# Single PSUM banks, pipelined rounding, two interleaved FFN units and decay within a chunk, in a retention block followed by a SwiGLU FFN

## The chip, the cores and the metric

One core of a Trainium2 chip. The metric is the time of one execution on the device in microseconds; a figure is the median of the runs named with it. Engines are named as in the profile: PE is TensorE (PEld its weight loads), DVE VectorE, ACT ScalarE, POOL GpSimd; SPq and ACTq are queues from which transfers are issued. A profile line gives start, duration, engine, line of the kernel, operation and tiles; in brackets stands how long the engine was idle before and what released it.

## The reference

Retention over 8 batches and 8 heads (576 positions, 64 per head), then an FFN over the 4608 tokens of 512 features. All products are fp32; the weights arrive as fp64.

```python
scores = scale * np.matmul(q, k.transpose(0, 1, 3, 2))
gamma = 1.0 - 2.0 ** (-5.0 - np.arange(H))
Dmat = np.where(rel >= 0, gamma[:, None, None] ** rel[None], 0.0)   # rel = pos_q - pos_k
x = np.matmul(scores * Dmat[None], v)            # then (B,H,S,D) -> (B*S, H*D)
xn = x / np.sqrt(np.mean(x * x, axis=-1, keepdims=True) + 1e-06) * rms_g
g = xn @ w_gate
out = (g / (1.0 + np.exp(-g)) * (xn @ w_val)) @ w_out
```

## The kernel before

A job is a batch and a pair of heads (32 jobs); a unit is 384 tokens of the FFN (12 units). An f is one of the 12 blocks of 128 of the 1536 hidden features: for each f a unit makes a gate product and a value product, and `h` is SiLU(gate) times value. `ret` holds a job's scores after the mask, `av` its values, `sd` the copies of its states (sums of k times v). An `attention_step(j)` computes scores of job j within chunks of 128 positions and per-chunk states, then the values of job j-1. FFN steps are issued between attention steps as soon as their tokens are there; a batch yields one or two units, so that attention steps come in runs where FFN work has run out. The weights (36 chunks) are rounded from fp64 words on VectorE with one step on ScalarE.

```python
psum = ctx.enter_context(tc.tile_pool(name="psum", bufs=4, space=PS))
def banks(name):                                   # two banks, one tile
    return psum.tile([P, 2, 512], F32, tag="ps", name=name)
...
def gate(u, f, hs):
    weights_to(2 * f + 4)                          # rounds chunks ahead of use
    ps = banks(f"gv_{u}_{f}")
    project(u, f, w_gate, ps[:, 0])
    t = ffn.tile([P, U], F32, tag="silu", name=f"silu_{u}_{f}", bufs=2)
    nc.scalar.activation(out=t, in_=ps[:, 0, :U], func=AF.Silu)
    hs[f] = t, ps[:, 1]                            # the value product goes to the second half
...
def attention_step(j):
    scores(j); states(j)          # PE
    values(j - 1)                 # PE, reads ret(j - 1)
    weigh(j)                      # DVE: ret = s * causal (2 buffers), sums; POOL: copies the states
    carried(j - 1)                # PE, reads the states and qT(j - 1)
    prepare(j + 2)                # DVE transposes q, k; POOL scales q and v
    load(j + 3)
...
def round_chunk(i):
    # DVE: e = exponent of hi ; ACT: e = Relu(e - 896)
    # DVE: e = min(e, 255) * 2**23 ; e = sign(hi) | e          <- need ACT's result
    # DVE: dst = mantissa of hi ; dst += lo * 2**-32           <- need nothing from ACT
    # DVE: dst = dst * 2**-20 * e
```

(Conditions on j, transfers and operands are cut.)

## Time and profile before

| | before |
|---|---|
| time, 3 runs | 1637.59 us (1637.22 to 1637.93) |
| PE / DVE / POOL busy | 84% / 23% / 8% |
| first gate product starts | 108.8 us |
| unit 0's output ends | 320.5 us |
| the value product's waits for the SiLU | 134.5 us, 139 times |

The page's lines for the busy shares and the wait stand in the prediction; the two times are read from TensorE's timeline.

```profile
L205 POOL COPY sd<-sum 64x256 f32<-64x256 f32 x64 | 26.3, 410 | 1063.2 <-DVE sum L202 1061.0
```

Read the two times as borders: up to 108.8 us TensorE has attention alone, to 320.5 us TensorE follows VectorE's rounding of weights, and after that TensorE is nearly full.

### The profile page before, as it was taken

How to read it: one execution, taken by the hardware profiler on the slowest of the kernel's cores; microseconds unless marked ns; L12 is line 12 of the kernel's file. 1: busy time of each engine (PE TensorE's matmuls, PEld its weight loads, DVE VectorE, ACT ScalarE, POOL GpSimd, SP SyncE). 2: the span in 40 equal slices, each digit the busy share in tenths (PEclk: the TensorE clock that was granted, in tenths of full speed). 3: DMA queues.
4: the chain of work that ended last, by engine and by line, in shares of the span. 5: the costliest groups of instructions: out<-in, count | busy, mean ns of one | idle time of the engine just before them, and what ended most of it. 6: DMA issues, size and time to landing. Idle time of an engine off the chain costs nothing.

```text
span 1638.6 us, 13258 instructions
## 1 busy us (share of the span) xinstructions
PE 1374.8 (84%) x5312; PEld 758.2 (46%) x5312; DVE 373.8 (23%) x772; ACT 160.4 (10%) x310; POOL 131.2 (8%) x180
## 2 busy tenths in 40 slices
PE   4555554879999999889999899889999999799998
PEld 3433221454444455555444544554444644354444
DVE  3754456241000211330000410230000300110000
ACT  0111111110000100100000100100000100100000
POOL 3320000030000100220000300120000200000000
PEclk9777775889999999999999999999999999799999
DMA  9761223150000210430000410230000100000000
GB/s 181 154 133 52 77 77 115 50 96 0 13 7 0 62 28 14 89 72 0 20 1 7 95 31 0 62 71 0 19 0 7 42 1 7 13 0 7 13 0 20
DMA packets 244349, 67.15 MB, mean 41 GB/s; under 512 B 225600, under 2 KB 238016, under 8 KB 244160
## 3 DMA queue, kind: packets, MB, share of 16 engines
q1 hardware_dynamic: 228928, 46.17, 14.0%
q10 hardware_dynamic: 15360, 20.14, 4.0%
q8 instruction: 42, 0.69, 0.2%
q14 instruction: 19, 0.16, 0.0%
HBM read 56.84 MB, written 9.44 MB: 40 GB/s over the span
## 4 chain that ended last, share of the span: by engine, by line
PE 74%; DVE 11%; ACT 6%; DMA 3%; SPq 3%; issue 2%; POOL 2%; ACTq 0%; DVEq 0%; POOLq 0%
PE gv L297 48%; PE out L322 22%; ACT silu L307 4%; SPq L116 2%; DMA kraw<-in_k_dram 2%; ACT exp L428 2%; DVE exp L432 1%; DVE ret L192 1%; DVE exp L429 1%; DVE exp L424 1%; PE s L171 1%; DVE kT L143 1%; PE av L215 1%; PE av L228 1%; ACT sq L255 1%
## 5 line engine op out<-in xcount | busy, mean ns | idle before, releaser
L297 PE MATMUL gv<-x,w_val 128*128 128x384 f32 x1152 | 427.3, 516 | 134.6 <-ACT silu L307 134.5
L297 PE MATMUL gv<-x,w_gate 128*128 128x384 f32 x1152 | 407.4, 498 | 26.8 <-DVE x L290 26.8
L322 PE MATMUL out<-w_out,h 128*128 128x512 f32 x864 | 386.5, 606 | 21.9 <-DVE w_out L442 21.9
L297 PEld LDWEIGHTS gv<-x,w_val 128*128 128x128 f32 x1152 | 215.4, 197 | 344.5 <-ACT silu L307 221.4
L297 PEld LDWEIGHTS gv<-x,w_gate 128*128 128x128 f32 x1152 | 223.6, 195 | 188.9 <-issue 25.2
L314 DVE TENSOR_TENSOR h<-silu,gv 128x384 f32<-128x384 f32 x144 | 79.8, 554 | 888.6 <-PE gv L297 888.6
L322 PEld LDWEIGHTS out<-w_out,h 128*128 128x128 f32 x864 | 165.7, 193 | 235.5 <-issue 195.9
L307 ACT ACTIVATE silu<-gv 128x384 f32<-128x384 f32 x144 | 70.7, 491 | 764.5 <-PE gv L297 739.4
L171 PE MATMUL s<-qT,kT 64*128 64x128 f32 (+1 forms) x640 | 57.4, 320 | 66.2 <-DVE ret L192 22.9
L205 POOL COPY sd<-sum 64x256 f32<-64x256 f32 x64 | 26.3, 410 | 1063.2 <-DVE sum L202 1061.0
L192 DVE TENSOR_TENSOR ret<-s,causal 128x768 f32<-128x768 f32 (+2 forms) x96 | 47.5, 542 | 167.4 <-PE s L171 166.3
L171 PEld LDWEIGHTS s<-qT,kT 64*128 64x128 f32 (+1 forms) x640 | 46.7, 212 | 80.0 <-issue 30.6
L328 ACT COPY o<-out 128x512 f32<-128x512 f32 x36 | 21.1, 586 | 376.0 <-PE out L322 376.0
L148 POOL TENSOR_TENSOR v<-v,gv 128x512 f32<-128x512 f32 x64 | 49.3, 790 | 29.2 <-DMA v<-in_v_dram 29.2
L215 PE MATMUL av<-ret,v 128*64 128x128 f32 (+1 forms) x640 | 51.1, 305 | 0.0
L145 POOL TENSOR_TENSOR qT<-qT,gq 128x576 f32<-128x576 f32 x32 | 45.0, 1405 | 56.4 <-DVE qT L143 49.9
L215 PEld LDWEIGHTS av<-ret,v 128*64 128x64 f32 (+1 forms) x640 | 42.2, 163 | 7.2 <-issue 5.9
L428 ACT ACTIVATE exp<-exp,least 128x512 f32<-128x512 uint32 x36 | 26.0, 721 | 176.1 <-DVE exp L424 176.1
L228 PE MATMUL av<-qT,sd 128*128 128x128 f32 (+1 forms) x256 | 37.1, 289 | 0.7 <-POOL sd L205 0.7
L239 ACT COPY x<-av 128x192 f32<-128x192 f32 (+1 forms) x80 | 23.4, 356 | 136.6 <-PE av L228 112.8
L228 PEld LDWEIGHTS av<-qT,sd 128*128 128x128 f32 x256 | 32.7, 200 | 3.4 <-POOL sd L205 1.1
L259 DVE TENSOR_TENSOR sq<-sq 128x768 f32<-128x768 f32 (+1 forms) x24 | 18.3, 761 | 62.6 <-ACT sq L255 62.2
(40 smaller groups left out, 359.4 us busy)
## 6 DMA issues: line engine op xcount, KB each, us to landing
qraw<-in_q_dram SPq DMA_DIRECT2D x128, 72.0 KB, 2.5
kraw<-in_k_dram SPq DMA_DIRECT2D x128, 72.0 KB, 2.7
out_dram<-o SPq DMA_DIRECT2D x36, 256.0 KB, 2.0
kn<-in_k_dram SPq DMA_DIRECT2D x64, 128.0 KB, 2.9
v<-in_v_dram SPq DMA_DIRECT2D x64, 128.0 KB, 2.8
w<-in_moe_w_gate_dram ACTq DMA_DIRECT2D x12, 512.0 KB, 3.8
w<-in_moe_w_val_dram ACTq DMA_DIRECT2D x12, 512.0 KB, 3.6
w<-in_moe_w_out_dram ACTq DMA_DIRECT2D x12, 512.0 KB, 3.5
```

The lines of the kernel that those rows point to most:

```text
L116: nc.sync.dma_start(out=t[r : r + SQ], in_=rows[i])
L145: nc.gpsimd.tensor_tensor(out=d["qT"], in0=d["qT"], in1=gq[:, hp], op=ALU.mult)
L148: nc.gpsimd.tensor_tensor(out=t, in0=t, in1=gv[:n, hp, cs].unsqueeze(3).to_broadcast([n, cs.stop - cs.start, 2, D]), op=ALU.mult,)
L171: nc.tensor.matmul(d["s"][blk][:n, e, o : o + n], lhsT=d["kT"][r, ck], rhs=d["qT"][r, ck], start=True, stop=True,)
L192: nc.vector.tensor_tensor(out=ret[:n, :, c0 * P : c0 * P + m * n].rearrange("p e (c k) -> p e c k", c=m), in0=s[blk][:n, :, o : o + m * n] ...
L215: nc.tensor.matmul(av[e * D : e * D + D, blk, o : o + n], lhsT=d["v"][:n, c, e], rhs=d["ret"][:n, e, c * P : c * P + n], start=(c in (0, A ...
L228: nc.tensor.matmul(av[:, blk, o : o + n], lhsT=sd[j % 2][:, c - 1], rhs=d["qT"][:, c * P : c * P + n], start=False, stop=(c in (AC - 1, NC ...
L297: nc.tensor.matmul(ps[:, :U], lhsT=w[:, c, f * P : f * P + P], rhs=x_of[u][:, c], start=(c == 0), stop=(c == NHP - 1),)
L307: nc.scalar.activation(out=t, in_=ps[:, 0, :U], func=AF.Silu)
L314: nc.vector.tensor_tensor(out=h, in0=t, in1=ps[:, :U], op=ALU.mult)
L322: nc.tensor.matmul(ps[s][:, :DM], lhsT=hs[f][:, s * P : s * P + P], rhs=w_out[:, f], start=(f == 0), stop=(f == NF - 1),)
L428: nc.scalar.activation(out=e.bitcast(F32), in_=e, func=AF.Relu, bias=least)
```

## The change

Its intent: gate, value, out and av each take one bank from a ring of four (scores keep two pairs), so that nothing waits for a neighbour in the same tile; the exponent of the next chunk is taken ahead, so that VectorE needn't wait for ScalarE; units 0 and 1 are interleaved from f = 6, so that TensorE has work while weights are rounded; the decay is counted from the start of each chunk, which shrinks the tables from 1152 + 20 to about 256 KB on the device side and frees SBUF for more buffers of `h` (14 to 20). To make room, `ret` goes from two buffers to one and q, k, v are prepared one step ahead, not two. Besides, the norm of a unit is issued a little later, the query scaling becomes two operations and the SiLU gets a third buffer. `LEAD` is the number of f that unit 0 is ahead, `WAHEAD` that of weight chunks loaded ahead. The core of the diff (its cuts are marked by `...`):

```diff
-    psum = ctx.enter_context(tc.tile_pool(name="psum", bufs=4, space=PS))
+    pairs = ctx.enter_context(tc.tile_pool(name="pairs", bufs=2, space=PS))
+    banks = ctx.enter_context(tc.tile_pool(name="banks", bufs=4, space=PS))
...
-        s, ret = d.pop("s"), att.tile([P, 2, S], F32, tag="ret", name=f"ret_{j}")
+        s, ret = d.pop("s"), att.tile([P, 2, S], F32, tag="ret", name=f"ret_{j}", bufs=1)
...
-            nc.vector.tensor_tensor(out=t[:, c], in0=part[:, c], in1=t[:, c - 1], op=ALU.add)
+            nc.vector.scalar_tensor_tensor(
+                out=t[:, c], in0=t[:, c - 1], scalar=gc[:, hp : hp + 1], in1=part[:, c],
+                op0=ALU.mult, op1=ALU.add,
+            )
...
-            nc.gpsimd.tensor_copy(out=sd[j % 2][r, :, r], in_=t[r])
+            nc.gpsimd.tensor_scalar(
+                out=sd[j % 2][r, :, r], in0=t[r], scalar1=gc[r, hp : hp + 1], scalar2=None,
+                op0=ALU.mult,
+            )
...
+        ps = bank(f"val_{u}_{f}")
         project(u, f, w_val, ps)
...
+        for f in range(NF):
+            yield from up(0, f)
+            if f >= LEAD:                       # LEAD = 6
+                yield from up(1, f - LEAD)
+        yield from down(0)
...
+        if j + 1 < len(jobs):
+            prepare(j + 1)
         if j + 2 < len(jobs):
-            prepare(j + 2)
+            load_kv(j + 2)
         if j + 3 < len(jobs):
-            load(j + 3)
+            load_qk(j + 3)
...
     def weights_to(n):
+            exponent(n_chunks + 1)
             round_chunk(n_chunks)               # inside: mantissa steps first, then ACT's result
-            if n_chunks + 2 < len(chunks):
-                load_chunk(n_chunks + 2)
+            if n_chunks + WAHEAD < len(chunks): # WAHEAD = 3
+                load_chunk(n_chunks + WAHEAD)
```

## The prediction

> **What bounds the kernel now.** I read the page's busy shares and 40 slices first, then the groups by line, then the timeline in four places: a steady stretch, the stretch in which the first unit's weights are rounded, a run of attention steps, and the end.
>
> ```profile
> PE 1374.8 (84%) x5312; PEld 758.2 (46%) x5312; DVE 373.8 (23%) x772; ACT 160.4 (10%) x310; POOL 131.2 (8%) x180
> PE   4555554879999999889999899889999999799998
> DVE  3754456241000211330000410230000300110000
> PEclk9777775889999999999999999999999999799999
> ...
> L297 PE MATMUL gv<-x,w_val 128*128 128x384 f32 x1152 | 427.3, 516 | 134.6 <-ACT silu L307 134.5
> L322 PE MATMUL out<-w_out,h 128*128 128x512 f32 x864 | 386.5, 606 | 21.9 <-DVE w_out L442 21.9
> ```
>
> TensorE sets the end, but not as one regime. In the first seven slices (to about 287 us) it is half busy at a clock of 0.6 to 0.8, because VectorE rounds weights; from there on it is 90% busy at a clock near 1.0. The groups name the largest wait: the value product waits 134.5 us for the SiLU. The steady timeline shows what that is:
>
> ```profile
> 458.17 2.85 PE L297 MATMUL gv<-x,w_val 128*128 128x384 f32 x8 [0.58 <-ACT silu L307]
> 460.85 2.74 PE L297 MATMUL gv<-x,w_gate 128*128 128x384 f32 x8
> 463.63 0.49 ACT L307 ACTIVATE silu<-gv 128x384 f32<-128x384 f32 x1 [5.52 <-PE gv L297]
> 464.18 2.85 PE L297 MATMUL gv<-x,w_val 128*128 128x384 f32 x8 [0.58 <-ACT silu L307]
> ```
>
> Each fp32 matmul is two records, so one product is x8. Gate and value together recur every 6.01 us. The value product needs nothing of the SiLU; it waits because both halves are one two-bank PSUM tile. The wait lists give 127 such waits of 0.58 us after 345 us, and 12 before it that sum to 60.8 us. The second kind is here:
>
> ```profile
> 159.26 0.42 DVE L424 TENSOR_SCALAR exp<-w 128x512 uint32<-128x512 uint32 x1
> 160.47 0.43 DVE L429 TENSOR_SCALAR exp<-exp 128x512 uint32<-128x512 f32 x1 [0.79 <-ACT exp L428]
> 163.33 0.42 DVE L424 TENSOR_SCALAR exp<-w 128x512 uint32<-128x512 uint32 x1
> ...
> 167.27 0.49 ACT L307 ACTIVATE silu<-gv 128x384 f32<-128x384 f32 x1 [2.76 <-DVE w_val L439]
> 167.81 4.81 PE L297 MATMUL gv<-x,w_val 128*128 128x384 f32 x8 [6.54 <-ACT silu L307]
> 172.46 2.74 PE L297 MATMUL gv<-x,w_gate 128*128 128x384 f32 x8
> ```
>
> A chunk of weights takes VectorE 4.07 us, 0.75 of it waiting for ScalarE. Two chunks, then a SiLU held behind ScalarE's weight load, then the value product, then its multiplication, run one after another: some 13.9 us for each f of unit 0. Last, attention steps in a run, warm:
>
> ```profile
> 678.72 1.42 PE L171 MATMUL s<-qT,kT 64*128 64x128 f32 x20
> 680.07 0.69 PE L181 MATMUL s<-v,kn 128*64 128x64 f32 x16
> 680.59 1.31 PE L215 MATMUL av<-ret,v 128*64 128x128 f32 x20
> 681.82 1.10 PE L228 MATMUL av<-qT,sd 128*128 128x128 f32 x8
> 682.86 1.42 PE L171 MATMUL s<-qT,kT 64*128 64x128 f32 x20
> ```
>
> A step is 4.14 us of TensorE and the next follows without a gap.
>
> **What the Trainium skill says.** "PSUM — Partial Sum Buffer", section "PSUM bank collisions raise a hardware error": two engines must not touch one bank in one quadrant together, while different banks run clean. So single-bank tiles lose this wait legally; the trace agrees that the wait (0.58) is just the SiLU (0.49) plus hand-over. "Perfetto Trace Analysis", section "Optimization Strategy": a repeated equal bubble on the engine that should be full can mean too few buffers; the 0.58 that recurs fits. "TensorE: Matmul & The Clock Gate", section "HAM oscillation": idle gaps over about 3.4 us bring the half clock back. The trace agrees: the value product takes 4.5 to 5.5 us after 6.5 us of idling, 2.85 otherwise. "SBUF — State Buffer", section "Who interferes with whom": VectorE and GpSimd share a port pair. The trace agrees in the attention start, where the same rounding operation takes 1.42 instead of 0.69 us while GpSimd runs.
>
> **The change part by part.**
>
> *Single banks.* Without the wait, eight matmuls follow at the 0.322 us seen inside a product: 2.58 us each, 5.16 for an f. The out product confirms the continuous rate (24 records in 10.3 us at 512 columns). Saving 6.01 - 5.16 = 0.85 us for each f in the steady part. ScalarE (0.49) and VectorE (0.55) per 5.16 us keep up, and a ring of four gives a bank back one whole f before it is needed. After the first stage there are 126 f left (12 x 12, less 12 of unit 0, less 6 moved forward), and some five have a norm or attention between gate and value and never waited: 121 x 0.85 = 103 us.
>
> *Rounding pipelined.* The 0.75 us wait goes: 3.32 us a chunk. The separate value bank takes the product out of the loop too. An f with two chunks then costs VectorE 6.64 + 0.3 (SiLU behind the weight load) + 0.55 = 7.5 us instead of 13.9.
>
> *Units 0 and 1 interleaved.* From f = 6 a slot holds an f of each unit, 10.3 us of TensorE against 8.1 of VectorE, so TensorE bounds it. The instruction order of the built kernel confirms this, and that one more attention step (nine, not eight) comes before the first gate.
>
> *The start, step by step.* The first gate started at 108.8 us. The tables shrink (1152 KB to 256 KB), the transposes are held to one step ahead, and one more step goes in; I set 110. f = 0 to 2, with a cold first product: 19 us, 129. f = 3 with one chunk: 6, 135. f = 4 and 5: 15, and 2 for the next unit's norm: 152. Six doubled slots: 12 x 5.16 + 1 = 63, 215. Ten chunks of w_out, in VectorE's order after the last multiplication: 33, 248, with TensorE mostly idle. Its last matmul and the two other row blocks: 22, **270**. In the kernel before, unit 0 ended at 320.5. Moreover 6 f of unit 1 (36 us at the old rate) and one attention step (4.1) are already done.
>
> *What attention pays.* `ret` goes from two buffers to one and q/k are prepared one step ahead instead of two. The built kernel shows the first multiplication of a step waiting for the value products of the step before. In a run of steps without FFN between, the loop is then: scores, states and values of the step on TensorE 3.2 us, weighing on VectorE 1.5, sums 0.95, one transpose 0.75, GpSimd's query scaling about 1.3 (1.405 for 576 columns, now 512 first), hand-overs 0.3: 8.0 us instead of 4.14. Cold, as in the first 100 us (scores 2.4, values 2.3), about 10.4. At the start VectorE and loading already held a step to about 10.5 us, so nothing is lost there. In the late part the order shows three runs, with 5 + 6 + 2 such waits: 13 x 4.6 (between warm 3.9 and cold) = 60 us. Against it stand the old kernel's own waits there (query scaling 13.4, and norm waits of about 12, as the squares leave the path of the next transpose): -25. Net **+35**.
>
> *GpSimd and VectorE details.* Two query scalings instead of one, and a scalar operand in sums and states: under 1 us a step, beside other work except in that loop.
>
> Sum: 270 + (1638.6 - 320.5) - 36 - 4 - 103 + 35 = 1480 us, 158 less.
>
> **Rivals.**
> (A) *The attention runs cost nothing.* For: they cost little now, and a loop may be broken if TensorE gets ahead by a step. Against: the wait is in the built order. Time: about 1445.
> (B) *The start stays bound by VectorE and loading.* Interleaving moves TensorE's work into the stage but takes nothing from VectorE, which has to round 36 chunks whatever the order (120 us at 3.32); if GpSimd's port or weight loading stretches a chunk back to 4, and SiLUs behind loads on ScalarE's queue stop the ring of banks, the stage ends near 305. For: ScalarE did wait 2.7 us behind loads each time. Against: with three staging buffers a load has two chunks of time, 6.6 us, against 3.6 to land. Time: about 1515.
> (C) *The bubble is replaced.* If four banks shared among gate, value, out and av bring a new wait on the multiplication, the 103 us halve: about 1530. Against: a bank has a whole f of slack.
>
> **Range and chances.** The 103 us are nearly arithmetic. The start (50 + 40 us) and the attention runs (+35) are each uncertain by some 30. Together: 1480, range 1440 to 1520. Even with half of all gains lost it is 1560, well below the 2% line at 1605. Faster 0.97, same 0.02, slower 0.01.
>
> **What would show it right or wrong.** Right: value products without any wait for the SiLU and 5.16 us per f; rounding at 3.3 us a chunk with no idle before its third step; first gate near 110, unit 0's last out near 270; TensorE's clock at 1.0 from about 155 us; a wait for query scaling or `ret` of about 4 us at each step of an attention run. Wrong: value or gate products that wait for a multiplication or copy (C), VectorE's chunks above 4 us or TensorE idle in the doubled slots (B), or attention runs at 4.1 us a step (A).

## The result, and the profile after

1505.24 us (1503.73 to 1509.79, 4 runs) against 1637.76 us before in the same rounds. The ratio is 0.9192 (95% interval 0.9169 to 0.9215). Ratios here are the mean time of one kernel's fast runs over that of the other's fast runs of the same rounds, so not quite the ratio of the medians quoted. All runs that are compared were fast (none lies over 0.6% above the fastest of its kernel).

The page of the changed kernel, in the same order as in the prediction: busy shares, slices, groups.

```profile
PE 1335.9 (89%) x5312; PEld 777.0 (52%) x5312; DVE 390.4 (26%) x772; ACT 160.8 (11%) x310; POOL 175.9 (12%) x212
PE   2557896999999995699999996599999999699999
PEclk9668995999999997899999998789999999699999
...
L307 PE MATMUL val<-x,w_val 128*128 128x384 f32 x1152 | 397.8, 489 | 3.5 <-ACT silu L317 3.0
L212 POOL TENSOR_SCALAR sd<-sum,gc 64x256 f32<-64x256 f32 x64 | 59.9, 937 | 1007.1 <-DVE sum L206 1004.2
L174 PE MATMUL s<-qT,kT 64*128 64x128 f32 (+1 forms) x640 | 68.9, 373 | 120.5 <-POOL qT L144 104.5
```

The value product's wait is gone: 134.5 us became 3.0. In its place stands a new largest wait of TensorE: the scores wait 104.5 us for GpSimd's scaled queries (18.9 before). And the copies of the states now take 937 ns each, against 410 before. The slices show where: late in the kernel the 16th, 17th, 25th, 26th and 35th have PE at only 0.5 to 0.7; these are the runs of attention steps.

The timeline of one steady stretch (start, duration, engine, line, what):

```profile
186.17 2.74 PE L307 MATMUL gate<-x,w_gate 128*128 128x384 f32 x8
188.75 2.74 PE L307 MATMUL val<-x,w_val 128*128 128x384 f32 x8
191.33 2.74 PE L307 MATMUL gate<-x,w_gate 128*128 128x384 f32 x8
193.91 2.74 PE L307 MATMUL val<-x,w_val 128*128 128x384 f32 x8
```

Starts are 2.58 us apart: 5.16 us an f where it was 6.01. The timeline of two steps in a run of attention steps is the counterpart:

```profile
594.88 2.49 PE L174 MATMUL s<-qT,kT 64*128 64x128 f32 x20 [5.01 <-POOL qT L144]
598.21 1.32 PE L225 MATMUL av<-ret,v 128*64 128x128 f32 x20
599.57 1.48 DVE L196 TENSOR_TENSOR ret<-s,causal 128x768 f32<-128x768 f32 x3 [6.69 <-PE av L225]
601.22 0.91 DVE L206 SCALAR_TENSOR_TENSOR sum<-sum,gc,s 128x64 f32<-128x64 f32 x3
602.12 0.78 DVE L139 STREAM_TRANSPOSE qT<-qraw 128x576 f32<-128x576 f32 x1
602.23 1.93 POOL L212 TENSOR_SCALAR sd<-sum,gc 64x256 f32<-64x256 f32 x2 [5.78 <-DVE sum L206]
604.25 1.54 POOL L144 TENSOR_TENSOR qT<-qT,gq 128x512 f32<-128x512 f32 x2
605.56 2.49 PE L174 MATMUL s<-qT,kT 64*128 64x128 f32 x20 [4.38 <-POOL qT L144]
```

Read it downwards: each line starts when the one above lets it. Scores and values on TensorE, then weighing (which waited for the values, `PE av L225`: the single buffer of `ret`), sums, transpose, then GpSimd's states *before* the query, then the query, then the next scores. This turn takes 10.7 us, the shortest after the first of a run; the others take up to 11.8 (first turns 9.2). In the run that the prediction shows it took 4.14 us without any wait.

Where the time went, by the borders of the stages:

| stage | before | after |
|---|---|---|
| to the first gate product | 108.8 us | 121.5 us (one more attention step in it) |
| from there to the end of unit 0 | 211.7 us | 162.3 us (six f of unit 1 in it) |
| from there to the end | 1318.1 us | 1220.1 us |

### The profile page after: what moved, and what is told of

Read it like the earlier page. It is cut to its first block, busy times and chain, and to the rows that moved or that the text cites. A ratio compares the mean times of both kernels' runs of the same rounds, so it can differ in the third digit from the quotient of the medians.

```text
span 1503.9 us, 13309 instructions
## 1 busy us (share of the span) xinstructions
PE 1335.9 (89%) x5312; PEld 777.0 (52%) x5312; DVE 390.4 (26%) x772; ACT 160.8 (11%) x310; POOL 175.9 (12%) x212
## 4 chain that ended last, share of the span: by engine, by line
PE 83%; DVE 9%; POOL 4%; DMA 2%; issue 1%; ACT 0%; ACTq 0%; SPq 0%; DVEq 0%; POOLq 0%
PE gate L307 24%; PE val L307 24%; PE out L331 24%; PE s L174 4%; PE av L225 3%; POOL sd L212 2%; DVE ret L196 2%; PE s L184 2%; POOL qT L144 2%; DVE sum L206 1%; DVE exp L475 1%; DMA v<-in_v_dram 1%; DVE exp L472 1%; DVE exp L449 1%; DVE w_out L478 0%
## 5 line engine op out<-in xcount | busy, mean ns | idle before, releaser
L307 PE MATMUL gate<-x,w_gate 128*128 128x384 f32 x1152 | 403.7, 494 | 18.4 <-DVE x L300 17.2
L307 PE MATMUL val<-x,w_val 128*128 128x384 f32 x1152 | 397.8, 489 | 3.5 <-ACT silu L317 3.0
L307 PEld LDWEIGHTS gate<-x,w_gate 128*128 128x128 f32 x1152 | 221.2, 193 | 177.0 <-issue 27.6
L307 PEld LDWEIGHTS val<-x,w_val 128*128 128x128 f32 x1152 | 219.9, 191 | 157.9 <-ACT silu L317 3.7
L323 DVE TENSOR_TENSOR h<-silu,val 128x384 f32<-128x384 f32 x144 | 79.8, 554 | 738.7 <-PE val L307 736.7
L212 POOL TENSOR_SCALAR sd<-sum,gc 64x256 f32<-64x256 f32 x64 | 59.9, 937 | 1007.1 <-DVE sum L206 1004.2
L174 PE MATMUL s<-qT,kT 64*128 64x128 f32 (+1 forms) x640 | 68.9, 373 | 120.5 <-POOL qT L144 104.5
L317 ACT ACTIVATE silu<-gate 128x384 f32<-128x384 f32 x144 | 70.7, 492 | 611.8 <-PE gate L307 598.7
L196 DVE TENSOR_TENSOR ret<-s,causal 128x768 f32<-128x768 f32 (+2 forms) x96 | 47.4, 549 | 251.8 <-PE av L225 249.3
L144 POOL TENSOR_TENSOR qT<-qT,gq 128x512 f32<-128x512 f32 x64 | 54.9, 877 | 13.3 <-DVE qT L139 10.8
L225 PE MATMUL av<-ret,v 128*64 128x128 f32 (+1 forms) x640 | 54.0, 318 | 0.1
L225 PEld LDWEIGHTS av<-ret,v 128*64 128x64 f32 (+1 forms) x640 | 45.3, 172 | 6.9 <-issue 6.9
L184 PE MATMUL s<-v,k 128*64 128x64 f32 x512 | 31.4, 291 | 0.1
```

The lines of the kernel that those rows point to most:

```text
L144: nc.gpsimd.tensor_tensor(out=t, in0=t, in1=gq[:, hp, :n].unsqueeze(1).to_broadcast([P, m, n]), op=ALU.mult)
L174: nc.tensor.matmul(d["s"][blk][:n, e, o : o + n], lhsT=d["kT"][r, ck], rhs=d["qT"][r, ck], start=True, stop=True,)
L184: nc.tensor.matmul(d["s"][1][e * D : e * D + D, 0, SC + c * D : SC + c * D + D], lhsT=d["k"][:, c, e], rhs=d["v"][:, c, e], start=True, st ...
L196: nc.vector.tensor_tensor(out=ret[:n, :, c0 * P : c0 * P + m * n].rearrange("p e (c k) -> p e c k", c=m), in0=s[blk][:n, :, o : o + m * n] ...
L212: nc.gpsimd.tensor_scalar(out=sd[j % 2][r, :, r], in0=t[r], scalar1=gc[r, hp : hp + 1], scalar2=None, op0=ALU.mult,)
L225: nc.tensor.matmul(av[blk][e * D : e * D + D, o : o + n], lhsT=d["v"][:n, c, e], rhs=d["ret"][:n, e, c * P : c * P + n], start=(c in (0, A ...
```

## The experiments

Twelve kernels ran, in three groups of four; each group shares its runs of the kernel before (medians 1640.44, 1640.81, 1639.99 us; the third reuses those of the first). The second group (e5 to e8) ran on another chip, so it is best compared by ratio. All gave the correct result; each time is the median of 4 runs.

| run | time | ratio to before (95%) |
|---|---|---|
| e1 before + single banks only | 1482.49 | 0.9044 (0.9017 to 0.9071) |
| e2 changed, units not interleaved | 1520.90 | 0.9273 (0.9250 to 0.9297) |
| e3 changed, two buffers of ret | 1455.62 | 0.8871 (0.8849 to 0.8893) |
| e4 changed, plain states | 1489.02 | 0.9074 (0.9054 to 0.9095) |
| e5 changed, no pipelining over chunks | 1502.49 | 0.9157 (0.9137 to 0.9177) |
| e6 changed, attention buffers of before | 1440.27 | 0.8779 (0.8764 to 0.8794) |
| e7 two ret, out by weight | 1436.28 | 0.8754 (0.8738 to 0.8770) |
| e8 all | 1424.07 | 0.8686 (0.8663 to 0.8709) |
| e9 changed, rounding wholly as before | 1519.32 | 0.9259 (0.9236 to 0.9283) |
| e10 best | 1414.64 | 0.8631 (0.8606 to 0.8656) |
| e11 before + three small edits | 1434.90 | 0.8753 (0.8732 to 0.8775) |
| e12 changed again | 1505.40 | 0.9178 (0.9152 to 0.9203) |

**e1: one part alone.** The ring of four single banks put into the kernel before, nothing else.

```diff
-    psum = ctx.enter_context(tc.tile_pool(name="psum", bufs=4, space=PS))
+    pairs = ctx.enter_context(tc.tile_pool(name="pairs", bufs=2, space=PS))     # scores
+    single = ctx.enter_context(tc.tile_pool(name="banks", bufs=4, space=PS))    # all else
-        ps = banks(f"gv_{u}_{f}")
-        hs[f] = t, ps[:, 1]
+        ps = bank(f"gate_{u}_{f}")          # and bank(f"val_{u}_{f}") in value()
```

> The kernel before with one part of the change alone: scores keep two pairs of banks, everything else (gate, value, out, av, norm) goes to a ring of four single banks; attention, rounding and order of units as before. Theory (the single banks pay through the value product's wait): 127 waits late x 0.85 = 108 us, and in unit 0 nine slow f go from 13.8 to about 9.0 us (two chunks of 4.07, 0.3, 0.55): 43 us more. About 1487 us, so FASTER than the whole change (1505), because the change pays for its gains in the attention steps. Rival (the banks' wait was only part, and interleaving and pipelined rounding carry the gain): about 1530, the 108 us alone or less.

Measured 1482.49 us. This part alone takes 158 us off, and is 23 us faster than the whole change. So the banks carry the gain, and the rest of the change taken together costs more than it brings. In e1's page the value product no longer waits for the SiLU at all:

```profile
L298 PE MATMUL val<-x,w_val 128*128 128x384 f32 x1152 | 397.1, 488 | 5.8 <-DVE w_val L443 5.8
```

Unit 0's slow f recur every 9.0 us, as expected, and unit 0 ends at 276.6 us instead of 320.5. The edit has a price too: scores have two pairs to themselves, where four were shared, and their waits for the weighing before (`<-DVE ret`) rise from 22.9 to 39.2 us.

**e2: interleaving undone.**

```diff
-    LEAD = 6
+    LEAD = 12
```

> The changed kernel with units 0 and 1 one after the other (the lead set to 12, which also gives the ring of h 14 buffers). Theory: in the doubled slots TensorE set the time (10.3 us each, 62), without them VectorE does (7.5 us an f, 45), and the six f of unit 1 (31 us) come later: plus 14 us, and a colder clock in the stage adds some: 1515 to 1525. Rival (interleaving is worth the whole six f, since the stage is bound by VectorE whatever is done): plus 31, 1536.

Measured 1520.90 us, 16 us more than the changed kernel (1505). The theory's 14 holds, the rival's 31 does not: of the six f moved forward only about half is gain, since the doubled slots lengthen the stage (unit 0's output starts at 227.4 us with them, at 207.1 without).

**e3: two buffers of ret.**

```diff
-att.tile([P, 2, S], F32, tag="ret", name=f"ret_{j}", bufs=1)
+att.tile([P, 2, S], F32, tag="ret", name=f"ret_{j}", bufs=2)
```

> The changed kernel with two buffers of ret again, nothing else. Theory (the loop of a lone attention step runs through ret): weighing no longer waits for the value products; the next transpose is then held by its own buffer (released by the last product of the step), so 1.5 us of the loop's 11.4 go, over 8 early and 13 late steps: minus 25 to 30, about 1478. Rival (the loop is held by preparing one step ahead and GpSimd, ret does not matter): within 5 us of the changed kernel.

Measured 1455.62 us: 50 us less, the sign and mechanism of the theory with nearly twice its size. From the timeline of TensorE in e3's counterpart run of steps, three lines that don't follow one another directly:

```profile
567.50 2.49 PE L174 MATMUL s<-qT,kT 64*128 64x128 f32 x20 [2.34 <-POOL qT L144]
576.20 1.42 PE L174 MATMUL s<-qT,kT 64*128 64x128 f32 x20 [2.98 <-POOL qT L144]
584.30 2.25 PE L174 MATMUL s<-qT,kT 64*128 64x128 f32 x20 [1.72 <-POOL qT L144]
```

In the late runs a step now recurs every 8.0 to 9.5 us instead of 10.7 to 11.8 (the first of a run every 7.2 instead of 9.2). Two things account for more than the estimate: of the 13 scores that wait, five ran in 1.42 us, where in the changed kernel all took 2.48 or 2.49; and the start gained 9 us (first gate at 112.5 instead of 121.5 us). That the shorter idling brought the clock back is a reading of these traces, not a test. In the lists of waits after 300 us the 13 waits for queries fall from 63.4 to 34.2 us.

**e4: states copied plainly.** The factor of a whole chunk is moved into the tables: values carry gamma to (128 - position), the mask gamma to -128 for each head. The result is the same.

```diff
-    t = ..., pairs.T[None] ** -pos[:, None, None], rows**P
+    t = ..., pairs.T[None] ** (P - pos)[:, None, None], rows**P
-                in1=causal[:n, :n].unsqueeze(1).unsqueeze(1).to_broadcast([n, 2, m, n]),
+                in1=causal[:n, hp, :, :n].unsqueeze(2).to_broadcast([n, 2, m, n]),
-            nc.gpsimd.tensor_scalar(out=sd[j % 2][r, :, r], in0=t[r], scalar1=gc[r, hp : hp + 1], ...)
+            nc.gpsimd.tensor_copy(out=sd[j % 2][r, :, r], in_=t[r])
```

> The changed kernel with the factor of a whole chunk moved out of GpSimd's copy of the states: the value table carries gamma to (128 - position) and the causal mask gamma to -128, so that the states are copied plainly as in the kernel before; same result. Theory (the multiplication with a scalar operand, 0.94 us against 0.41 for the copy, delays the query scaling that each attention step waits for): 1.1 us x 21 steps = 23 us, about 1482. Rival (GpSimd's time lies beside other work): no change. The loop without it should be near 10.3 us.

Measured 1489.02 us, 16 us less. The copies take 394 ns, and the late steps recur every 10.1 to 10.6 us (10.3 expected); the scores' waits fall from 104.5 to 79.2 us. The total falls less than 23 us; part of it was probably lost at the start, where new waits for loading (4.6 us) appear and the first gate comes 5 us earlier, not 9.

**e5: no pipelining over chunks**, and **e9: the old order inside a chunk as well.**

```diff
 e5:
-            exponent(n_chunks + 1)
+            exponent(n_chunks)
             round_chunk(n_chunks)
-    WAHEAD = 3
+    WAHEAD = 2
 e9, besides: the two steps on e (min/mult, sign) ahead of the two steps on dst again
```

> The changed kernel with a chunk's exponent taken just before its rounding again, and two chunks loaded ahead instead of three. Theory (each chunk then costs VectorE 0.75 us of waiting for ScalarE, which counts only where VectorE sets the time: the five chunks of f 3 to 5 and the ten of w_out; the attention start and the doubled slots have room): plus 11 us, about 1516. Rival (all chunks lie on the path): 0.75 x 36 = 27 us, about 1532.

> The run without pipelining again, and now the order of the steps inside a chunk as in the kernel before too (the step that needs ScalarE's result comes second, not fourth). In the run without pipelining the chunk stayed at 3.19 us, since two steps that need nothing from ScalarE already covered its 0.72 us. Theory (the gain of rounding is all in the order inside a chunk): a chunk goes to 4.05 us, and over five chunks of f 3 to 5 and ten of w_out that is 15 x 0.8 = 12 us: about 1515. Rival (the attention start pays as well): up to 12 + 9 x 0.8 = 20 us, 1523; or nothing, 1503, if the stage's slack takes it.

e5 missed: 1502.49 us, no slower than the changed kernel (the intervals overlap). Lines of one chunk in e5, then in e9, up to the first step of the next, say why; the page calls the steps by the tile that they write.

```profile
237.69 0.42 DVE L449 TENSOR_SCALAR exp<-w 128x512 uint32<-128x512 uint32 x1
238.02 0.42 DVE L465 TENSOR_SCALAR w_out<-w 128x512 uint32<-128x512 uint32 x1
238.14 0.72 ACT L453 ACTIVATE exp<-exp,least 128x512 f32<-128x512 uint32 x1 [2.47 <-DVE exp L449]
238.47 0.69 DVE L469 SCALAR_TENSOR_TENSOR w_out<-w,w_out 128x512 f32<-128x512 uint32 x1
239.08 0.42 DVE L472 TENSOR_SCALAR exp<-exp 128x512 uint32<-128x512 f32 x1
240.87 0.42 DVE L449 TENSOR_SCALAR exp<-w 128x512 uint32<-128x512 uint32 x1
```

```profile
237.10 0.42 DVE L449 TENSOR_SCALAR exp<-w 128x512 uint32<-128x512 uint32 x1
237.56 0.72 ACT L453 ACTIVATE exp<-exp,least 128x512 f32<-128x512 uint32 x1 [3.35 <-DVE exp L449]
238.31 0.43 DVE L465 TENSOR_SCALAR exp<-exp 128x512 uint32<-128x512 f32 x1 [0.79 <-ACT exp L453]
241.17 0.42 DVE L449 TENSOR_SCALAR exp<-w 128x512 uint32<-128x512 uint32 x1
```

In e5 the two steps on the mantissa (`w_out`) stand between the exponent and the step that needs ScalarE, and they cover its 0.72 us: no wait, and a chunk every 3.18 us. With the pipelining of the changed kernel it is 3.31 us. In e9 the wait of 0.79 us is back, a chunk takes 4.07 us, and the time is 1519.32 us: in ratios 0.9259 against 0.9157, 17 us, between the theory's 12 and the rival's 20. So the order of steps inside a chunk is enough for the gain of this part, and with it the pipelining over chunks brought nothing. Pipelining with the old order was not run; it may do the same alone.

**e6: the attention buffers of before** (ret two, q transposed three, k three, v four buffers, prepared two steps ahead; lead 10 for the space, so this run changes two things).

```diff
-        if j + 1 < len(jobs):
-            prepare(j + 1)
         if j + 2 < len(jobs):
-            load_kv(j + 2)
+            prepare(j + 2)
         if j + 3 < len(jobs):
             load_qk(j + 3)
+            load_kv(j + 3)
```

> The changed kernel with the attention buffers of the kernel before: two of ret, three of qT, q, k and v prepared two steps ahead (k three, v four buffers); the lead is 10 instead of 6, so that it fits (20 buffers of h become 16), which by the run without interleaving costs some 10 us. Theory (the attention loop cost the change about what the kernel with single banks alone was faster by, and more): the late steps in a run go from 11.3 us to about 4.9 (GpSimd: states 1.9, query 1.55, values 1.4), 13 x 6.4 = 83 us, the start a further 10: about 1425 with the lead's 10 us. Rival (ret alone was the loop, the rest is GpSimd and loading): no better than two buffers of ret (1456) plus 10.

Measured 1440.27 us: 65 us less than the changed kernel, but 15 above the expected 1425. It shows about what the change had paid in attention for its space. The late part did what was expected (its waits of scores are 17 us instead of 63). The start did not: the first gate product starts at 118.4 us, since scores wait there for the two pairs of banks (39.7 us in the whole trace `<-DVE ret L196`, 12.5 of it after 300 us). The theory had only counted queries, not banks.

**e7: unit 0's output by weight**, on e3: each chunk of w_out serves all three row blocks while VectorE rounds the next.

```diff
+            if u == 0:
+                for f0 in range(NF):
+                    for s in range(U // P):
+                        yield u, DM, lambda s=s, f0=f0: contract(u, s, f0, f0 + 1, ps)
+                return
```

> The changed kernel with two buffers of ret, and unit 0's three row blocks of the output product taken together, weight by weight, in three banks: a chunk of w_out is used by all three while VectorE rounds the next. Theory (TensorE idles 20 us in this stage because only one block follows the rounding): 31 us of products then fit beside 33 us of rounding: minus 18 to 20 us against two buffers of ret alone, about 1437. Rival (the stage is bound by something else, such as the cold clock, or the three open banks stop the ring): 5 us or less.

Measured 1436.28 us, 19 us less than e3. Two lines of each timeline, the changed kernel's first, then e7's:

```profile
238.14 2.07 PE L331 MATMUL out<-w_out,h 128*128 128x512 f32 x2 [1.24 <-DVE w_out L478]
241.45 2.07 PE L331 MATMUL out<-w_out,h 128*128 128x512 f32 x2 [1.24 <-DVE w_out L478]
```

```profile
237.46 2.84 PE L331 MATMUL out<-w_out,h 128*128 128x512 f32 x6 [0.47 <-DVE w_out L483]
240.77 2.84 PE L331 MATMUL out<-w_out,h 128*128 128x512 f32 x6 [0.47 <-DVE w_out L483]
```

The chunk's interval of 3.31 us stays; six records go into it instead of two.

**e8: all together**, without interleaving (lead 12 for the space).

> All together: single banks and pipelined rounding of the change; attention buffers of the kernel before; plain states; output of unit 0 by weight; no interleaving of the units (lead 12, for the space). Expected: 1425 of the run with two steps ahead, minus 9 for plain states (GpSimd at 3.8 us a step is below TensorE's 4.14), plus 5 for the lead, minus 20 for the output by weight: about 1401. If the parts overlap instead, about 1425.

Measured 1424.07 us; a miss by 23 us from the sum of parts, as e6 had missed; the other value, 1425 if the parts overlap, came true. The late part has few waits of scores left (19 us), but the first gate starts at 119.1 us.

**e10: the best version found.** The changed kernel with one-step-ahead preparation kept, two buffers of ret, three of the transposed q, plain states, output by weight, lead 9. Its edits are those of e3, e4 and e7, `LEAD = 9`, and:

```diff
-            t = att.tile([P, S], F32, tag=nm + "T", name=f"{nm}T_{j}")
+            t = att.tile([P, S], F32, tag=nm + "T", name=f"{nm}T_{j}", bufs=3 if nm == "q" else 2)
```

> The changed kernel with two buffers of ret, three of qT, plain states, unit 0's output by weight, lead 9 for the space. Against the run with two buffers of ret and output by weight (1436): the loop of an attention step loses GpSimd's extra 1.1 us and the transpose's wait for the last product (0.5 to 1.8), together 1.6 to 2.5 over 13 late steps (21 to 33 us), less at the start, where loading binds (0 to 10); the lead costs 3 x 2.7 = 8, less what the output by weight makes up. About 1415. Rival (the loop is by now held by something else): 1436 to 1440.

Measured 1414.64 us, as expected: 14% below the kernel before and 6% below the change.

**e11: three small edits on the kernel before:** the banks of e1, the new order inside a chunk, the output by weight of e7.

> The kernel before with three small edits: single banks, the new order of steps inside a chunk (no pipelining over chunks), unit 0's output by weight. From 1482: 0.75 us x 28 chunks on the path (17 in unit 0's f, 11 of w_out) = 21 us, and 18 us for the output by weight: about 1443, well below the whole change. Rival (the attention start or the norms take up the slack): 1465.

Measured 1434.90 us, a little better than expected. It has no interleaving, no pipelining over chunks and none of the decay's rework, and beats the change by 70 us.

**e12: the control.**

> The changed kernel itself, as a control beside these three: 1503 to 1510.

Measured 1505.40 us.

## Why the prediction was right, and where its sizes were off

The measured 1505 us lies in the range (1440 to 1520), 25 us above the predicted 1480. By the prediction's own steps:

- **Single banks.** Right, to the hundredth: 5.16 us an f, waits of the value product 3.0 us. Rival C (a new wait in the ring) did not come. e1 confirms the part on its own. There are eight banks before and after; only their division into tiles changed.
- **Rounding.** The predicted 3.32 us a chunk was measured at 3.31. The cause was not as put: the prediction credited pipelining, and e5 and e9 show that the order inside a chunk, which the change also altered, is enough.
- **Interleaving.** From the first doubled slot (159.2 us) to the first output (227.4) it took 68 us, predicted 63: one wait of 2.8 us for a SiLU that stood behind a weight load, and a value product at half clock after it (4.54 us, granted clock 0.51). From the first gate to the doubled slots it took 38 us, predicted 42. The sign "clock at 1.0 from about 155 us" came only in part: the granted clock was 0.98 from 150.4 to 225.6 us, but 0.58 while w_out is rounded (227.4 to 261 us).
- **The start: the first mis-sized term.** The first gate came at 121.5 us, not 110. The prediction said that nothing is lost there, since VectorE and loading held a step to 10.5 us anyway. Steps recurred every 11.6 us (scores at 25.4 and 106.8 us, seven steps apart): here too the loop over ret and the queries was the bound (two buffers of ret alone bring the first gate to 112.5, e3), and it was longer than the estimated 10.4.
- **The loop itself: the second.** Predicted 8.0 us warm and 10.4 cold, 4.6 above a free step of 4.14 on average; measured 10.7 to 11.8 in the late runs. In the turn shown, the three products on TensorE take 4.65 us (3.2 counted, warm), weighing and sums 2.6 (2.45), and from there to the next scores 3.4 us (2.35 for transpose, query and hand-overs). The sum had no term for the states on GpSimd: two copies took 0.85 us before, about as long as the transpose beside them; with the scalar operand two of them take 1.93 us and stand before the query. "Under 1 us a step, beside other work except in that loop" was thus right in its exception; e4 puts it at 16 us in all. The 13 waits were foreseen in number from the instruction order. From one start of scores to the next these turns took 86 us more than 13 free steps, against 60 predicted (the waits alone sum to 63.4, but the steps ran cold as well). The old kernel's ten lengthened steps after 320 us had taken 36 us more, against 25 taken off. So the term is +50 where +35 was predicted; the late part as a whole was off by only 10, and what made up the other 5 was not traced.
- **Rivals.** A (attention runs cost nothing) is refuted by 104.5 us of waits, and e3 and e6 show that the buffers are the main reason. B (the start stays bound by rounding and loading) did not come: a chunk stayed at 3.31 us and unit 0 ended at 283.8 us, not 305. The attention start was late, but by its own loop.

In sum: 14 us of the 25 came up to the end of unit 0, 10 after it. What the prediction did not see at all is that the part it called net +35 made the change slower than its own first part alone. Nothing new was needed for that: the expectation of e1 gets 1487 us from the 127 waits and the durations of unit 0 that the prediction had read, but the prediction never summed one part without the others. One reading was off without consequence: of the seven slices said to have a clock of 0.6 to 0.8, the first had 0.96.

## What to carry to other kernels

Before taking a bundle of changes, sum each part on the kernel before by itself: here one part gave 158 us and the bundle 132. Buffers saved in one stage are paid in another: walk round the loop that a single buffer closes, with every instruction that its engines do in order, also those that seem to be beside it. And where one engine waits for another's short step, look first whether steps of the same item can be put in between; this was enough here, and pipelining over items added nothing to it.

## What the Trainium skill lacked or had wrong

- GpSimd's cost by kind of operand: "GPSIMD Engine Reference" has measured costs for two-tensor operations, but none for a scalar for each partition. Such a multiplication of 64x256 fp32 took 937 ns on average in the changed kernel, a copy of the same shape 410 ns in the kernel before and 394 ns in e4.
- "TensorE: Matmul & The Clock Gate", section "HAM oscillation", gives idle gaps above about 3.4 us as what brings the half clock; its next section, "A second HAM failure mode", says that frequent short idles can do it too, but gives no length. Here the half clock also came after shorter gaps, and not each time. In e3 a single gap of 3.00 us after a stretch of steady work left scores at a granted clock of 0.50 (2.49 us) in one run of steps and at 1.00 (1.42 us) in the two others. In the changed kernel a gap of 2.80 us was followed by a value product at 0.51 (4.54 us).
- "PSUM — Partial Sum Buffer" tells that different banks may be used at once, but not what two banks in one tile cost in a program: the second bank's writer waited for the first bank's reader, 0.58 us, 127 times, after 345 us, and no longer once each bank was its own tile.
- No page was found that tells to put independent steps of the same item between another engine's step and its use: they covered ScalarE's 0.72 us (a chunk took 3.18 us in e5, 4.07 in e9).
